# A PSUM bank turn moved on by one, and a small DMA issued earlier, in a fused Fourier-mixing and GELU kernel

## The chip, the core and the metric

The kernel runs on one core of a Trainium2 chip. The metric is the device time of one execution in microseconds. The median of several executions is given; one further execution was recorded by the hardware profiler, and all times inside the kernel are from that one.

## The reference

Two blocks stand one behind the other. The first takes, for each of 8 batches, a two-dimensional Fourier transform of a 3008 by 256 array and keeps the real part. The second multiplies each of the 24064 rows by a 256 by 2048 matrix, applies the quick GELU and multiplies by a 2048 by 256 matrix. All is in 32-bit floating point.

```python
batch, seq, dim = (8, 3008, 256)
n_tokens, d_model, d_ff = (24064, 256, 2048)

X = np.fft.fft(x, axis=1)
X = np.fft.fft(X, axis=2)
attn = X.real.astype(np.float32)

h = attn.reshape(B * S, D) @ w_in
g = h * (1.0 / (1.0 + np.exp(-1.702 * h)))
return (g @ w_out).astype(np.float32)
```

## The kernel before, in words

**The mathematics as tiled.** The transform along the sequence (3008 = 47 × 64) is made in two stages of small matrix products. The first stage (`mix_first` for batch 0, `mix1` for later ones) leaves its results in DRAM, from where `fill` brings them back. The second stage (`stage2`) makes blocks `pq` of cosine and sine parts. The transform along the feature axis is folded into the first weight matrix: `fold_w(n)` multiplies a quarter of it (`wst`) by a cosine and sine matrix and copies the two products from PSUM into a quarter of `wcs[0]` and `wcs[1]`. The second weight matrix is kept in `wo`, with differences of its blocks in `wt`. One row of each block, the Nyquist row `nb`, is handled apart: row 0 of `wcs[1]` holds its weights. `first_row(n)` copies these into columns `af1` and `af2`, and in the later steps row 0 of `wcs[1]` has to be zero. `no_row(c0)` writes 1024 zeros there with a DMA from a table in DRAM (L497).

**Steps.** After an opening written out line by line (L839 to L918) a single loop runs over steps t (L977). A step is one batch, block, half block and pair of hidden columns; NP = 8 pairs make a group. The first eight steps (t < 8) have a form of their own: `hidden(t)` computes two PSUM banks, `pa` (with the cosine weights) and `pb` (sine weights), ScalarE copies `pa` to SBUF, VectorE's `rows(t)` makes sums and differences from both (L566, L569, L557; L557 is the last reader of `pa`), ScalarE's `activate(t)` applies GELU, and `product(t)` multiplies by the second weights three steps later into the banks o0 and o1. `product` and most other matrix products are issued by the helper `halves`, L184, so their lines in the profile are told apart by tile names: `o` the products, `psw` of `fold_w`, `psf` of `first_row`, `psr` of `rotate`, `psn` of `nyquist`. From t = 8 on `begin(t, cs)` takes the place of `hidden`, into a tile `x`, and `begin(t, 1)` reads `wcs[1]` with its row 0.

**The weights' preparation.** In the opening and in the first steps the weights, which come as 64-bit numbers, are turned into 32-bit ones, quarter by quarter: `squares`, `low_up`, `low_down` on ScalarE (L410, L420, L425), `clamp` on POOL (L415), `high` on VectorE (L443 to L445), `finish_in` and `finish_out` on POOL (L457, L465). `differences` (L475) is on POOL, `small_weights` (L687) on VectorE. This stands between the work of the steps on the same engines.

**PSUM.** [...] Two, o0 and o1, hold the products. The other six are handed out by `bank`: without a tag it takes the first of the list `spare` and puts it at the end, so that a bank comes round after six calls. The list starts as b0, b1, b2, o2, o3, o4. A call has to wait until the readers of the bank's former contents are done. At t = NP − 3 = 5 the turn is broken: `spare` is cut down to the banks whose names begin with o, in their present order, and b2 (L980), and `hidden(5)` takes b0 for `pa` and b1 for `pb` by name (L523). From t = 7 on `middle(t)` takes b0 or b1 by name.

**Order of calls around the change.** In the opening: `warm(3)`, `fold_w(0)` (two banks), `warm(1)`, `rotate`, `stage2(0, 0)` (two banks), `first_row(0)`, `fold_w(1)` (two). In the loop: two banks for each `hidden(t)`; one for `nyquist` at t = 0; one for `first_row` at t = 1, 4 and 6; two for `fold_w(2)` at t = 3 and `fold_w(3)` at t = 5; one for `rotate` at the end of t = 4.

**Queues.** [...] SP's queue issues most DMAs. At the end of step 3 it gets, from the list `extra`, `load_matrices` (four DMAs of the first stage's matrices, L324), three `turn`s (DRAM to DRAM, for batch 1) and four calls of `load_x` (two DMAs each, L205), which fill the tile `xt` that `fold1` on POOL first reads at t = 11. In step 4 it then gets `no_row(0)`. `no_row(1024)` follows in step 7.

Of the kernel before, what the change touches and what calls it, by code (L numbers as in the profile page):

```python
# [112 lines left out]
def kernel(ctx: ExitStack, tc, x, w_in, w_out, tab1, tab2, out):  # L113
# [53 lines left out]
    spare = ["b0", "b1", "b2", "o2", "o3", "o4"]  # L167

    def bank(name, tag=None):
        if tag is None:  # L170
            tag = spare.pop(0)
            spare.append(tag)
        if tag in ("o0", "o1"):
            return o_banks[int(tag[1])]
        return (rest if tag[0] == "o" else psp).tile([128, 512], F32, tag=tag, name=name)
# [5 lines left out]
    def halves(out, lhs, rhs, **how):  # L181

        for c0 in (0, 64):
            nc.tensor.matmul(out[c0:c0 + 64], lhsT=lhs[:, c0:c0 + 64], rhs=rhs, skip_group_check=True, **how)  # L184
# [164 lines left out]
    def stage2(b, blk):  # L349

        pq, t4 = pqp.tile([128, 2, 512], F32, tag="pq", name="pq"), t4t[b]
        pqt[b, blk] = pq
        m = m2 if b else m2f
        ps = [bank("ps2") for _ in range(NU)]
        for cs in range(2):
            for h in range(2):
                for g in range(4):
                    for u in range(NU):
                        rows, at = slice(64 * u, 64 * u + 64), cs * 256 + h * 128
                        nc.tensor.matmul(ps[u][32 * g:32 * g + 32, at:at + 128], lhsT=m[rows, cs, h * RUN:(h + 1) * RUN],  # L360
                                         rhs=t4[rows, 4 * blk:4 * blk + 4, cs * H + 32 * g:cs * H + 32 * g + 32],
                                         start=(cs == h == 0), stop=True, skip_group_check=True)
        for u in range(NU):
            for cs in range(2):

                nc.vector.transpose(free(pq[:], cs * 512 + u * RUN, [256, 2], [NU * RUN, 4], [1, RUN]),
                                    free(ps[u][:], cs * 256, [128, 2], [32, 4], [1, 32]))
# [50 lines left out]
    def low_up(key, lo=0, n=1024):  # L418

        nc.scalar.activation(pre[key][2][:, lo:lo + n].bitcast(F32), raw[key][:, lo:lo + n, 0], ACTF.Copy, scale=2.0 ** -29,  # L420
                             bias=2.0 ** 23)

    def low_down(key, lo=0, n=1024):
        r = pre[key][2][:, lo:lo + n]
        nc.scalar.activation(r, r.bitcast(F32), ACTF.Copy, bias=-2.0 ** 23)  # L425

    def bounds(key, end=True):
        prepare(key)
        squares(key, nc.scalar)
        clamp(key)  # L430
        low_up(key)
        if end:
            low_down(key)
# [53 lines left out]
    def first_row(n):  # L487

        ps = bank("psf")
        for f in range(4 * n, 4 * n + 4):  # L490
            halves(ps[:, f:f + 1], wcs[1][0:1, f * 128:f * 128 + 128], twos[:], start=True, stop=True)
        nc.scalar.copy(af2[:, 4 * n:4 * n + 4], ps[:, 4 * n:4 * n + 4])
        nc.scalar.activation(af1[:, 4 * n:4 * n + 4], ps[:, 4 * n:4 * n + 4], ACTF.Copy, scale=0.5)


    def no_row(c0):
        nc.sync.dma_start(out=wcs[1][0:1, c0:c0 + 1024], in_=tab1[127:128, n0 + 4:n0 + 1028])  # L497
# [22 lines left out]
    def hidden(t):  # L520

        n = width(t)
        pa, pb = (bank(name, f"b{i}" if t == NP - 3 else None) for i, name in enumerate(("pa", "pb")))  # L523
        for ps, cs in ((pa, 0), (pb, 1)):
            for i in range(2):
                halves(ps[:, i * 256:i * 256 + n], *operands(t, cs, i), start=(i == 0), stop=(i == 1))
        v = sp.tile([128, 512], F32, tag="v", name="v")
        nc.scalar.copy(two(v[:], n), two(pa[:], n))
        vb[t] = v, pa, pb
# [47 lines left out]
    def middle(t):  # L577

        b, blk, hh, p = steps[t]
        n = width(t)  # L580
        x = xb[t] = bank("x", f"b{t % 2}")
        for i in range(2):
            f = 2 * p + i
            nc.scalar.activation(x[:, i * 256:i * 256 + n], nbt[b, blk][:, hh * 256:hh * 256 + n], ACTF.Copy,  # L584
                                 scale=af1[:, f:f + 1])

    def begin(t, cs=0):

        n = width(t)
        for i in range(2):  # L590
            halves(xb[t][:, i * 256:i * 256 + n], *operands(t, cs, i), start=False, stop=(cs == 1))
# [315 lines left out]
    squares(out0, nc.scalar)  # L907
    stage2(0, 0)
    first_row(0)
    low_up(out0)  # L910
    low_down(out0)
    high(out0)
# [9 lines left out]
    def at(t, fn, *args):  # L922
        extra.setdefault(t, []).append((fn, args))
# [9 lines left out]
    rows_at = {1: 1, 4: 2, 6: 3}  # L933
    for t, c in ((0, 2), (1, 3)):
        at(t, load_out, c, nc.sync)
    at(3, load_matrices)
    if B > 1:
        for k in range(3):
# [38 lines left out]
    for t in range(n + LAG):  # L977
        if t < NP:
            if t == NP - 3:
                spare[:] = [tag for tag in spare if tag[0] == "o"] + ["b2"]  # L980
            if t == NP - 1:
                middle(NP)
            hidden(t)
            if t == NP - 1:
                begin(NP)
                no_row(1024)
            if t == 4:
                no_row(0)
            if t == 0:
                low_up(in2)  # L990
                nyquist(0, 0)
                low_down(in2)
            if t in rows_at:
                first_row(rows_at[t])
            if t >= LAG and t != LAG + 1:
                product(t - LAG, 0, None)
            if t == LAG:
                product(1, 0, None)
            if t == 5:
                bounds(("out", 2))  # L1000
            if t == 6:
                low_down(("out", 3))
            if t:
                activate(t - 1)
            if t == 3:
                bounds(("in", 3))
            if t == 5:
                bounds(("out", 3), False)
            if t in early:
                fold_w(early[t])  # L1010
            rows(t)
            if t == NP - 1:
                doubled(NP)
                middle(NP + 1)
        else:
            after, special = (any(fn in (mix1, stage2) for fn, _ in extra.get(k, ())) for k in (t - 1, t))
            if t < n:
                begin(t, 1)
            if t == NP:
                activate(t - 1)  # L1020
            if t < n:
                forward(t)
            if after and t + 1 < n:
                middle(t + 1)
            opening = (t - LAG) % NP == 0 and t >= NP + LAG
            one, other = (t - LAG, (1, 2, 4, 7)), (t - LAG - 1, (5, 6, 3))
            if opening:
                small_products(*other)
            cut = 0 if opening and not after else 3 if after else 2
            product(t - LAG, 0, cut)  # L1030
            if after:
                small_products(one[0], one[1][:1])
                small_products(other[0], () if opening else other[1][:1])
            if t + 1 < n:
                begin(t + 1)
            if not opening:
                small_products(other[0], other[1][after:])
            product(t - LAG, cut, 6 if t - LAG == last else None)
            small_products(one[0], one[1][after:])
            swap(t - LAG - 2)  # L1040
            if t < n:
                backward(t)
            if t + 1 < n:
                doubled(t + 1)
            if t < n:
                activate_back(t)
                sums(t, nc.gpsimd)
            if t + 2 < n and not special:
                middle(t + 2)
            combine_small(t - LAG - 1)  # L1050
            if t - LAG == last:
                product(last, 6, None)
            sums(t - 1, nc.vector)
            deeper(t - 2, 0)
            deeper(t - 3, 1)
        if t == NP:
            psu.close()
            low = ctx.enter_context(tc.tile_pool(name="low", bufs=1, space=PS))
            pot["low"] = low.tile([128, 3 * 512], F32, tag="low", name="low")
        if t >= LAG:  # L1060
            combine(t - LAG)
            combine_last(t - LAG - 2)
            turn_last(t - LAG - 3, 0)
            turn_last(t - LAG - 4, 1)
        if t >= NP:
            spare[:] = [f"b{t % 2}"] * special + ["b2"]
        for fn, args in extra.get(t, ()):
            fn(*args)
# [28 lines left out]
```

## Time and profile before

| what | us |
|---|---|
| median of 3 runs | 1861.46 (1861.33 to 1863.06) |
| the profiled execution | 1861.87 |
| its span, first to last instruction | 1860.1 |
| TensorE working (99% of the span) | 1842.7 |
| VectorE working (82%) | 1516.6 |
| ScalarE working (62%) | 1145.5 |
| POOL working (52%) | 966.8 |
| mean granted clock of TensorE | 0.997 of full |

The span leaves out 1.8 us that lie around the first and the last instruction. In the profile PE is TensorE's matmuls and PEld its loads of weights, DVE is VectorE, ACT ScalarE, POOL GpSimd and SP the engine that issues DMAs. A line such as "o<-big,wo" names the tile written and the tiles read. In a list of waits, "PE pb L184 <- DVE t L347: 2.6, 1, 2.6" says that matmuls into `pb` waited for an instruction of VectorE at line 347 for 2.6 us in total, once, the longest 2.6. Matmuls are pipelined and their ends are modelled, so the distance from one start to the next is the better measure of what a group costs. The eight first steps lie between 38.9 and about 88 us of the span.

### The profile page before, as it was taken

Reading aid. Unit: us, or ns where it says so; the run is one execution under the profiler, and the core shown is the slowest. Engines: PE = TensorE matmul, PEld = TensorE weight load, DVE = VectorE, ACT = ScalarE, POOL = GpSimd, SP = SyncE. Lnnn points to the kernel's source line nnn. Section 1 sums busy time; section 2 is a strip of 40 time slices with the busy share of each in tenths; the row PEclk is TensorE's granted clock in tenths of the full one; section 3 lists DMA queues with packets and bytes.
Section 4 is the critical chain, followed back from the end, with each engine's and each line's share of the span. In section 5 each row is a group of like instructions: output and inputs, shape, how many; then the busy total and the mean of one; then the engine's idle time right before and its main releaser. Section 6 shows DMA issues by size and latency. Waiting matters only on the chain.

```text
span 1860.1 us, 56075 instructions
## 1 busy us (share of the span) xinstructions
PE 1842.7 (99%) x23718; PEld 1402.6 (75%) x23718; DVE 1516.6 (82%) x2222; ACT 1145.5 (62%) x2240; POOL 966.8 (52%) x1053
## 2 busy tenths in 40 slices
PE   8999999999999999999999999999999999999998
PEld 4577777777777777777777777777777777778776
DVE  6778788888788877987789878888888888878874
ACT  5656665666666566666665666656666666656663
POOL 4676345844367443773347643486445754434442
PEclk9999999999999999999999999999999999999999
DMA  8721340224112250113302232021411111100111
GB/s 285 175 61 34 78 74 19 63 57 95 26 27 64 57 93 19 52 45 86 65 13 57 52 86 52 17 77 35 101 31 25 36 46 36 31 19 13 23 20 24
DMA packets 149691, 105.31 MB, mean 57 GB/s; under 512 B 106041, under 2 KB 130649, under 8 KB 148880
## 3 DMA queue, kind: packets, MB, share of 16 engines
q1 hardware_dynamic: 146608, 99.68, 23.4%
q8 instruction: 187, 3.06, 0.7%
q10 hardware_dynamic: 2832, 2.05, 0.4%
q14 instruction: 64, 0.52, 0.1%
HBM read 64.41 MB, written 48.05 MB: 60 GB/s over the span
## 4 chain that ended last, share of the span: by engine, by line
PE 91%; DVE 4%; POOL 2%; ACT 1%; DMA 1%; issue 1%; SPq 0%; DVEq 0%; ACTq 0%; POOLq 0%
PE x L184 33%; PE o L184 25%; PE low L677 24%; PE o L677 4%; PE ps L255 2%; PE ps L360 1%; DVE big L643 1%; DVE big L443 1%; ACT x L584 1%; DMA xt<-in_x_dram 1%; DMA big<-in_moe_w_in_dram 0%; DVE big L444 0%; DVE big L557 0%; DVE big L778 0%; PE po L184 0%
## 5 line engine op out<-in xcount | busy, mean ns | idle before, releaser
L614 POOL TENSOR_TENSOR big<-big 128x256 f32<-128x256 f32 (+1 forms) x376 | 347.6, 925 | 832.6 <-ACT big L606 714.0
L184 PE MATMUL x<-pq,wcs 128*64 128x256 f32 (+1 forms) x6016 | 771.4, 377 | 1.2 <-ACT x L584 0.3
L643 DVE TENSOR_TENSOR big<-big 128x512 f32<-128x512 f32 (+1 forms) x736 | 623.8, 862 | 31.3 <-PE low L677 14.4
L184 PE MATMUL o<-big,wo 128*64 128x256 f32 (+1 forms) x4800 | 622.8, 376 | 0.0
L184 PEld LDWEIGHTS x<-pq,wcs 128*64 128x64 f32 x6016 | 409.7, 137 | 191.5 <-issue 15.0
L184 PEld LDWEIGHTS o<-big,wo 128*64 128x64 f32 x4800 | 343.0, 137 | 148.8 <-issue 1.8
L596 ACT ACTIVATE g<-x 128x512 f32<-128x512 f32 (+1 forms) x376 | 221.7, 590 | 373.8 <-PE x L184 372.5
L557 DVE TENSOR_TENSOR big<-g,x 128x512 f32<-128x512 f32 (+2 forms) x440 | 253.7, 588 | 196.8 <-ACT big L599 196.3
L677 PE MATMUL low<-big 128*64 128x128 f32 (+1 forms) x5888 | 382.8, 270 | 0.0
L584 ACT ACTIVATE x<-nb,af 128x256 f32<-128x256 f32 (+1 forms) x752 | 352.7, 469 | 12.2
L677 PEld LDWEIGHTS low<-big 128*64 128x64 f32 x5888 | 337.5, 137 | 29.2
L615 POOL TENSOR_TENSOR big<-big 128x256 f32<-128x256 f32 (+1 forms) x376 | 359.1, 955 | 0.0
L599 ACT ACTIVATE big<-x 128x512 f32<-128x512 f32 (+1 forms) x376 | 220.4, 586 | 198.7 <-PE x L184 169.3
L606 ACT ACTIVATE big<-big 128x512 f32<-128x512 f32 (+1 forms) x376 | 231.9, 617 | 40.5 <-DVE big L557 38.7
L677 PE MATMUL low<-big,wo 128*64 128x128 f32 (+1 forms) x2944 | 220.2, 270 | 0.1
L677 PEld LDWEIGHTS low<-big,wo 128*64 128x64 f32 x2944 | 171.6, 137 | 3.2 <-DVE big L643 0.4
L622 DVE TENSOR_TENSOR big<-big 128x512 f32<-128x512 f32 (+1 forms) x188 | 157.6, 838 | 6.5
L621 DVE TENSOR_TENSOR big<-big 128x512 f32<-128x512 f32 (+1 forms) x188 | 136.4, 725 | 5.5 <-POOL big L614 5.5
L778 DVE TENSOR_TENSOR big<-big,low 128x512 f32<-128x512 f32 (+3 forms) x184 | 109.1, 610 | 3.5
L677 PEld LDWEIGHTS o<-big,wo 128*64 128x64 f32 x1472 | 92.2, 137 | 25.0
L677 PE MATMUL o<-big,wo 128*64 128x128 f32 (+1 forms) x1472 | 110.0, 270 | 0.0
L227 POOL TENSOR_TENSOR xt<-xt 111x510 f32<-111x510 f32 x56 | 81.0, 1447 | 4.4
(95 smaller groups left out, 959.5 us busy)
## 6 DMA issues: line engine op xcount, KB each, us to landing
out_dram<-os SPq DMA_DIRECT2D x284, 64.0 KB
t<-Td SPq DMA_DIRECT2D x22, 512.0 KB
Td<-xt SPq DMA_DIRECT2D x56, 192.0 KB
xt<-in_x_dram SPq DMA_DIRECT2D x14, 512.0 KB
xt<-Xr SPq DMA_DIRECT2D x14, 512.0 KB
nb<-Nd SPq DMA_DIRECT2D x23, 256.0 KB
out_dram<-os SPq DMA_DIRECT2D x96, 56.0 KB
Xr<-in_x_dram SPq DMA_DIRECT2D x7, 752.0 KB
```

The source lines that it names most:

```text
L184: nc.tensor.matmul(out[c0:c0 + 64], lhsT=lhs[:, c0:c0 + 64], rhs=rhs, skip_group_check=True, **how)
L557: nc.vector.tensor_tensor(free(out, at + m - 1, [by, 2], [RUN, blocks], [-1, m]), *ins, op=op)
L584: nc.scalar.activation(x[:, i * 256:i * 256 + n], nbt[b, blk][:, hh * 256:hh * 256 + n], ACTF.Copy, scale=af1[:, f:f + 1])
L596: nc.scalar.activation(two(g[:], n), two(xb[t][:], n), ACTF.Copy, scale=2.0)
L599: nc.scalar.activation(front(t), two(xb[t][:], width(t)), ACTF.Gelu_apprx_sigmoid)
L606: nc.scalar.activation(back(t), back(t), ACTF.Gelu_apprx_sigmoid)
L614: eng.tensor_tensor(right(t, S1, n), left(t, A21, n), right(t, A22, n), op=ALU.add)
L615: eng.tensor_tensor(left(t, S3, n), left(t, A11, n), left(t, A21, n), op=ALU.subtract)
L621: eng.tensor_tensor(s2, s1, a11, op=ALU.subtract)
L622: eng.tensor_tensor(s4, a12, s2, op=ALU.subtract)
L643: nc.vector.tensor_tensor(out, i0, i1, op=how)
L677: nc.tensor.matmul(o, lhsT=lhs, rhs=rhs, start=first_in, stop=(p == NP - 2), skip_group_check=True)
```

## The change

Two things are changed in the kernel. Behind `first_row(0)` in the opening, the first entry of `spare` is put at its end without being used, so that each later call takes the bank one place further on. And `no_row(0)` is no longer called in step 4 but put on the list of step 3, ahead of `load_matrices`.

```diff
     squares(out0, nc.scalar)
     stage2(0, 0)
     first_row(0)
+    spare.append(spare.pop(0))
     low_up(out0)
     low_down(out0)
     high(out0)
...
     for t, c in ((0, 2), (1, 3)):
         at(t, load_out, c, nc.sync)
+    at(3, no_row, 0)
     at(3, load_matrices)
     if B > 1:
         for k in range(3):
...
             if t == NP - 1:
                 begin(NP)
                 no_row(1024)
-            if t == 4:
-                no_row(0)
             if t == 0:
                 low_up(in2)
                 nyquist(0, 0)
```

## The prediction

> **What bounds the kernel now.** I read the page's engine table first, then TensorE's waits over the whole run, then the chain of waits, the order of time and the clock by stretches around the one place that these lead to.
>
> ```profile
> span 1860.1 us, 56075 instructions
> PE 1842.7 (99%) x23718; PEld 1402.6 (75%) x23718; DVE 1516.6 (82%) x2222; ACT 1145.5 (62%) x2240; POOL 966.8 (52%) x1053
> ...
> PE ps L312 <- DVE first L292: 3.0, 2, 2.3
> PE warm L330 <- DVE wcs L843: 2.7, 1, 2.7
> PE pb L184 <- DVE t L347: 2.6, 1, 2.6
> PE psw L184 <- POOL wst L457: 0.9, 2, 0.5
> PE pa L184 <- ACT af L493: 0.4, 1, 0.4
> PE x L184 <- ACT x L584: 0.3, 2, 0.2
> ```
>
> TensorE bounds the kernel: it works for 99% of the span, and all that it waits is these few lines, some 10 us. Behind 66 us only the last line (0.3 us) is left. So what TensorE loses in the opening is never caught up, and what it gains there should reach the end. Of the three large waits, two lie before 15 us and wait for the first input. The third, 2.6 us in one piece, ends at 64.70 us:
>
> ```profile
> 61.05 1.06 PE L184 MATMUL pa<-pq,wcs 128*64 128x256 f32 x8
> 64.70 1.97 PE L184 MATMUL pb<-pq,wcs 128*64 128x256 f32 x8 [2.59 <-DVE t L347]
> 66.44 5.61 PE L184 MATMUL o<-big,wo 128*64 128x256 f32 x32
> ...
> 77.73 3.67 PE L184 MATMUL o<-big,wo 128*64 128x256 f32 x32
> ...
> 63.00:63.20 0.20, 0.00 (x0) 0.00 (x0) 0.20 (x2) 0.20 (x1) 0.20 (x1) 1.00 0.16 41
> 63.80:64.20 0.40, 0.00 (x0) 0.00 (x0) 0.37 (x2) 0.40 (x1) 0.40 (x1) 0.50 0.03 5
> 69.70:70.00 0.30, 0.30 (x4) 0.15 (x2) 0.30 (x1) 0.00 (x0) 0.30 (x1) 0.50 1.08 109
> 70.40:70.60 0.20, 0.20 (x6) 0.14 (x4) 0.17 (x2) 0.00 (x0) 0.20 (x1) 0.92 0.85 82
> ```
>
> The first four lines are TensorE in order of time (start, length). The others are stretches: length, then the busy time of PE, PEld, DVE, ACT and POOL, then the granted clock. During the wait the clock falls to 0.50 and comes back only at about 70.4 us. The same 32 product matmuls take 5.4 us behind the wait and 3.5 us later. The wait costs about twice what the list of waits says.
>
> **Which wait it is.** This is step t=5, `hidden(5)`: `pa` ran, `pb` waited. I wrote out the turn of `spare` by hand. Before the change, the calls of step 4 take b1 and b2 (`hidden(4)`), o2 (`first_row(2)`) and o3 (`rotate`). `hidden(5)` has its banks fixed by name: b0 for `pa`, b1 for `pb`. So `pb` of step 5 goes into the bank of `pa` of step 4, whose last reader is `rows(4)`'s reversed sum, L557, on VectorE:
>
> ```profile
> 61.23 1.22 DVE L445 SCALAR_TENSOR_TENSOR big<-big 128x1024 uint32<-128x1024 uint32 x1
> 62.37 0.68 DVE L566 TENSOR_TENSOR big<-v,pb 128x512 f32<-128x512 f32 x1
> 62.97 0.86 DVE L569 SCALAR_TENSOR_TENSOR dif<-nb,af,pb 128x256 f32<-128x256 f32 x2
> 63.87 0.69 DVE L557 TENSOR_TENSOR big<-pa,dif 128x512 f32<-128x512 f32 x1
> 64.47 0.16 DVE L347 COPY t<-psr 128x8 f32<-128x8 f32 x1
> ```
>
> L557 ends at 64.56 and the weight load of `pb` starts at 64.67, 0.11 us later. The profile names L347, which ended last (64.63), but that copy reads o3, which `pb` doesn't touch. The same 0.11 us stands between `rows(0)`'s L557 (end 44.50) and `hidden(2)`'s weight load (44.61), where there is no L347.
>
> [...] everything behind `pb` stands too, though `product(2)` needs nothing that is late. [...] 1.6 us of idling (62.0 to 63.6) sufficed, and it took 5.7 us of work to get it back. [...]
>
> **The bank turn, step by step.** One `pop` and `append` costs no instruction. Written out, step 4 now takes b2, o2, o3, o4, and `fold_w(2)` of step 3 has b0 and b1. Both banks of `hidden(5)` were then last read by that fold's copies to SBUF, which end at 58.42 and 59.28. `pa` and `pb` need not wait.
> - Idling: `pb` would start a group's time (0.87 us) after `pa`, at 61.92, instead of 64.70: 2.78 us.
> - `pb` itself: 64.70 to 66.44 is 1.74 us, at full clock 0.87: 0.87 us.
> - `product(2)`: 66.44 to 71.87 is 5.43 us; the same at 77.73 took 3.51 and at 83.73 3.45, mean 3.48: 1.95 us.
>
> The sum is 5.60 us. A check: 5.7 us of work at clock 0.50 lose 2.85, against 0.87 + 1.95 = 2.82.
>
> Six other allocations get other predecessors, and none waits. `fold_w(1)` (34.81) takes banks of `warm` and of `rotate`, copied by 33.45. `hidden(0)` takes the banks of `stage2`, whose transposes it needs anyhow. The Nyquist row (40.75) takes `first_row(0)`'s, read by 35.57, and `pa` of `hidden(1)` takes `fold_w(0)`'s, read by 32.6. All the other places keep their predecessor of six places before, the 0.39 us wait at 44.65 included. The first bank of `fold_w(3)` now waits for `pb` of step 4, read by L569 until 63.83. `hidden(6)`'s second waits for `pa` of step 4 (64.56).
>
> **What is late next.** TensorE arrives 5.6 us earlier, and each supplier must keep up:
> - `product(2)` at 62.79: activations done by 53.4, weights (`finish_out(1)`) by 59.3.
> - `fold_w(3)` at 66.27: needs `wst` from POOL (L457), ready at 65.00 whatever TensorE does. Slack 1.27 us. Its bank has 2.4.
> - `hidden(6)` at 69.70: needs ScalarE's copies of `fold_w(3)`. ScalarE works without a gap from 61.03 to 68.96, then idles 5.71 us. The copy would be wanted at 74.66 − 5.60 = 69.06. Slack 0.10 us, the tightest of all. If it is missed, it costs what is missed, say 0.3 us, with no loss of clock.
> - `product(4)` at 78.1: weights from POOL's `finish_out(2)`, which can follow `differences(0)` at 71.07 and end by 73.6.
> - `finish_out(3)` can start at 77.4, as POOL is free from 76.5.
> - VectorE begins `rows(5)` at 64.63, as soon as it is free, instead of 66.78, and then waits for `hidden(6)` as before.
>
> From t=6 on every engine idles for TensorE (4.49 us VectorE, 5.71 ScalarE, 4.61 POOL), so their work moves with it.
>
> **The zeros.** The 4 KB DMA of `no_row(0)` costs TensorE nothing by itself. It moves on SP's queue from behind `load_x` (issued at 67.88) to ahead of `load_matrices` (48.20), past the four matrix loads, three `turn`s and four `load_x` calls (eight DMAs). It has to wait until `hidden(3)`'s `pb` matmuls have read the row, about 48.32. So SP waits 0.12 us and issues for 0.3: all behind it is issued some 0.4 to 0.6 us later. The next that need it are `fold1` on POOL at 109.35 (103.7 after the change), while DMA traffic fades out at about 81. So it is hidden by 20 us. The reader of the zeros is `begin(8, 1)`: at 87.18 before, at 81.58 after. Left in its old place, the row would stand behind the loads of x that fade out at 81, with under 1 us to spare. Bounds: I cost the move at 0, its worth as a guard is 0 to 1 us, and its harm at most 0.6 us if a load did matter. Nothing is moved past on POOL's queue.
>
> **The sum.** The profiled execution took 1861.87 us (span 1860.1): minus 5.60 gives 1856.27. The median of the runs is 1861.46, 0.41 lower: 1855.86. I say 1856.0. About 0.2% (3.7 us) can be told from no change.
>
> **Rivals.**
> - A, the sum above: 1856.0, own range 1855.1 to 1857.0 (0.3 us at ScalarE's copy, 0.6 us at the loads, a little less from the 0.3 us waits). Chance 0.86.
> - B, the wait goes and the half clock stays, or a late supplier returns as much: then only 2.78 us is won, 1856.0 + 2.82 = 1858.8. [...] Against: 0.50 appears only inside this wait and until 70.4; neighbours at 0.39 to 0.50 us kept 1.00. Chance 0.06.
> - C, no gain: the named releaser L347 is the true one, and `pb` still stands until 64.7: 1861.5. For it: the name and 0.04 us between its end and the load. Against: the banks, and the 0.11 us seen twice. Chance 0.03.
> - D, slower: TensorE runs into `fold_w(3)` before `wst` is there, because POOL's L457, now beside other VectorE work, ends late. A stall of s there costs s, and once it is some 1.6 us long it brings its own half clock, 2.85. The gain is used up when s + 2.85 passes 5.6, that is, s over 2.75, L457 over 4.0 us late; 5 us late gives 1861.46 + 0.98 = 1862.4, and from 7.7 us late (s = 6.45) the loss can be told from no change. Against: only 0.4 us of L457 now lies beside `rows(5)`. Chance 0.05.
>
> **How the numbers follow.** A's range, widened towards B and by the 1.7 us over which the runs spread, gives 1854.9 to 1858.2, leaving out most of B, C and D. Faster over 0.2% is A and the little of B that wins more than its 2.78 us (which lies within 0.2%): 0.86 + 0.02 = 0.88. Within: C, the rest of B and 0.02 of D, 0.03 + 0.04 + 0.02 = 0.09. Slower: the rest of D, 0.03.
>
> **What would show it.** In the profile after, the list of TensorE's waits lacks the 2.6 us line, the clock stays at 1.00 between 62 and 71 us, `product(2)` starts near 62.8 and takes 3.5, and the last `x` groups of the opening come 5.6 us earlier. SP's L497 stands ahead of L324, near 48.4. The forecast is wrong if a new TensorE wait over 1 us stands at `psw` or `pa` near 66 to 70 us, or if the gain is seen at 80 us and lost by the end.

## The result, and the profile after

| what | before | after |
|---|---|---|
| median of 12 runs each, us | 1861.15 (1860.58 to 1863.06) | 1857.03 (1855.82 to 1858.42) |
| the profiled execution, us | 1861.87 | 1857.22 |
| its span, us | 1860.1 | 1855.4 |

The medians differ by 4.1 us or 0.22%; the ratio is 0.9977 (95% interval 0.9968 to 0.9986), so the changed kernel is faster. TensorE's waits over the whole span of the changed kernel, in the same columns as before:

```profile
PE ps L312 <- DVE first L292: 2.9, 1, 2.9
PE warm L330 <- DVE wcs L843: 2.7, 1, 2.7
PE psw L184 <- POOL wst L457: 1.3, 3, 0.5
PE pa L184 <- ACT af L493: 0.4, 1, 0.4
PE x L184 <- ACT x L584: 0.4, 2, 0.2
```

The 2.6 us of `pb` are gone and nothing over 0.5 us has come in their place. TensorE and SP follow in order of time, then one stretch (length, busy time of PE, PEld, DVE, ACT and POOL, the granted clock, the busy share of the DMA engines, GB/s). The clock was 1.00 in each of the ten stretches of 1 us from 62 to 72 us:

```profile
62.01 1.06 PE L184 MATMUL pa<-pq,wcs 128*64 128x256 f32 x8
62.90 1.03 PE L184 MATMUL pb<-pq,wcs 128*64 128x256 f32 x8
63.77 3.62 PE L184 MATMUL o<-big,wo 128*64 128x256 f32 x32
67.22 3.60 PE L184 MATMUL psw<-wst,small 128*64 128x512 f32 x16
...
76.59 1.03 PE L184 MATMUL pa<-pq,wcs 128*64 128x256 f32 x8
...
49.31 0.28 SPq L497 DMA_DIRECT2D wcs<-in_tab_dram  x1
49.65 1.69 SPq L324 DMA_DIRECT2D w<-in_tab_dram  x4
...
66.00:67.00 1.00, 1.00 (x12) 0.64 (x10) 0.99 (x3) 1.00 (x2) 1.00 (x1) 1.00 1.00 303
```

From `pa` of step 5 to `pa` of step 7 it is 76.59 − 62.01 = 14.58 us. Before, the second of these started 81.24 − 61.05 = 20.19 us behind the first:

```profile
81.24 1.03 PE L184 MATMUL pa<-pq,wcs 128*64 128x256 f32 x8
```

The difference is 5.61 us, the prediction's 5.60. But the spans differ by 4.7 and the medians by 4.1. For the first gap, look at VectorE's first work on the weights, before and after:

```profile
21.69 1.23 DVE L412 TENSOR_TENSOR big<-big 128x1024 f32<-128x1024 f32 x1 [1.79 <-DMA big<-in_moe_w_in_dram]
```
```profile
22.62 1.23 DVE L412 TENSOR_TENSOR big<-big 128x1024 f32<-128x1024 f32 x1 [1.78 <-DMA big<-in_moe_w_in_dram]
```

The first quarter of the weights landed 0.93 us later in the profile after, and all behind it moved along. The change issues nothing so early. In ten profiles this start lies between 21.56 (filled3) and 22.80 us (row_only), 22.43 in a second profile of the kernel before, so it is how executions differ. The second gap, 5.6 us in two profiles against 4.1 us in the medians, is what the experiments had to explain.

### The profile page after: what moved, and what is told of

It is laid out like the page before. It is cut to its first block, busy times and chain, and to the rows that moved or that the text cites. A ratio compares the mean times of both kernels' runs of the same rounds, so it can differ in the third digit from the quotient of the medians.

```text
span 1855.4 us, 56074 instructions
## 1 busy us (share of the span) xinstructions
PE 1840.3 (99%) x23718; PEld 1400.7 (75%) x23718; DVE 1521.0 (82%) x2222; ACT 1146.7 (62%) x2240; POOL 972.2 (52%) x1053
## 4 chain that ended last, share of the span: by engine, by line
PE 92%; DVE 3%; POOL 2%; ACT 1%; DMA 1%; issue 1%; SPq 0%; DVEq 0%; POOLq 0%; ACTq 0%
PE x L184 33%; PE o L184 26%; PE low L677 24%; PE o L677 4%; PE ps L255 2%; PE ps L360 1%; DVE big L643 1%; DMA xt<-in_x_dram 1%; ACT x L584 1%; PE psw L184 0%; PE pa L184 0%; DMA big<-in_moe_w_in_dram 0%; DVE big L778 0%; PE po L184 0%; PE pb L184 0%
```

## The experiments

Theory 1 is the prediction's. The other theories are stated in the expectations. Five rounds were timed for each kernel, with the kernel before beside it on the same chip. Its medians were 1861.26 in the first four, 1861.49 in the next four and 1861.45 in the last three.

| run | median, us | against before (95% interval of the ratio) |
|---|---|---|
| turn_only | 1858.68 | 0.9984 to 0.9997 |
| row_only | 1861.77 | 0.9992 to 1.0008 |
| filled5 | 1861.40 | 0.9992 to 1.0009 |
| before_again | 1861.14 | 0.9992 to 1.0008 |
| filled3 | 1860.26 | 0.9985 to 1.0001 |
| swapped | 1862.37 | 0.9998 to 1.0014 |
| act_row | 1857.61 | 0.9971 to 0.9987 |
| best | 1857.15 | 0.9965 to 0.9985 |
| after_again | 1856.88 | 0.9965 to 0.9985 |
| best_again | 1856.85 | 0.9965 to 0.9985 |
| filled1 | 1859.64 | 0.9984 to 1.0000 |

**turn_only: the bank turn without the earlier zeros.**

```diff
     first_row(0)
+    spare.append(spare.pop(0))
     low_up(out0)
```

> The bank turn alone, the zeros left in step 4. Theory 1 (the turn carries the whole gain: 2.8 us of idling and 2.8 us of half clock at pb of step 5): 1857.0 us, as the full change, within 0.5; no TensorE wait over 0.5 us behind 16 us. Theory 2 (the earlier zeros are needed once TensorE is early): a wait of 0 to 1 us at the first x matmuls that read the sine weights, near 82 us, 1857.0 to 1858.0.

Measured: 1858.68, which is 2.58 us under the kernel before beside it, where the full change won 4.12. TensorE in order of time, its waits behind 66 us, and two stretches in columns as above:

```profile
78.69 3.62 PE L184 MATMUL o<-big,wo 128*64 128x256 f32 x32
84.20 0.98 PE L184 MATMUL x<-pq,wcs 128*64 128x226 f32 x8 [1.89 <-DMA wcs<-in_tab_dram]
...
PE x L184 <- DMA wcs<-in_tab_dram: 1.9, 1, 1.9
...
82.00:83.00 1.00, 0.31 (x4) 0.00 (x0) 0.97 (x2) 0.64 (x1) 1.00 (x1) 1.00 0.78 78
83.00:84.00 1.00, 0.00 (x0) 0.00 (x0) 1.00 (x2) 0.00 (x0) 1.00 (x2) 1.00 0.09 8
```

The wait of `pb` is gone with the turn alone, but `begin(8, 1)` now waits 1.9 us for the zeros, which SP issued at 70.2 behind the loads of x. The matmuls start only when the DMA engines, busy to 83 us, have run empty. Theory 2 was right in its place; its size, "0 to 1", was too small. Zeros that come early enough are what makes the turn's gain whole. Five of the 21 executions lie at 1860.56 to 1861.62 and the others under 1859.4. Those five may have lost clock behind the new wait as well; the profiled one did not, so this is not shown.

**row_only: the earlier zeros without the turn.**

```diff
+    at(3, no_row, 0)
     at(3, load_matrices)
...
-            if t == 4:
-                no_row(0)
```

> The earlier zeros alone, the bank turn as before. Theory 1: 1861.2 us, as before, with the 2.6 us wait of pb and the half clock behind it as they were. Theory 3 (holding SP for the zeros delays the loads behind it, and this is what brings the gain down from 5.6 to 4.1 us): 1862 to 1863 us.

No difference from before is seen (1861.77 against 1861.26, the interval holds 1), and the profile has the 2.6 us wait of `pb` again. While TensorE is late, nobody needs the zeros early. Theory 3 needs some 1.5 us, 5.6 less 4.1, and the interval just reaches that far. But in the full profile after, no engine waits for the loads behind the zeros, and act_row below speaks against it.

**act_row: the turn, the zeros in step 4 but from ScalarE's queue.**

```diff
     def no_row(c0):
-        nc.sync.dma_start(out=wcs[1][0:1, c0:c0 + 1024], in_=tab1[127:128, n0 + 4:n0 + 1028])
+        (nc.sync if c0 else nc.scalar).dma_start(out=wcs[1][0:1, c0:c0 + 1024], in_=tab1[127:128, n0 + 4:n0 + 1028])
...
     first_row(0)
+    spare.append(spare.pop(0))
     low_up(out0)
```

> The bank turn, with the zeros left in step 4 but issued from ScalarE's queue instead of SP's. If the zeros were late because they stood behind the loads of x in SP's own rings: they land within some us, no wait of x for them, 1857.0 us as the full change. If any DMA is late while the 16 engines are full with loads: a wait of 1 to 2 us at x again, 1858.7.

`x` does not wait for the zeros, and the median is 1857.61. They were late because of where they stood on SP's queue. This run doesn't tell apart whether SP's wait at `load_x` or the transfers ahead of them did it: ScalarE issued at 59.8, SP in turn_only at 70.2. The run also speaks against Theory 3: SP isn't held for the zeros here, and yet the gain is 3.9 us and not 5.6.

**before_again: the kernel before, as a control.**

> The kernel before, unchanged, as a control with a profile of its own. Theory 1: 1861.2 us; the wait of pb near 2.6 us and product of step 2 at half clock again. Theory 4 (the depth of the loss at half clock varies from run to run, so that the gain over many runs is less than in the one profile): the 5.4 us of that product are shorter in this profile, between 3.5 and 5.4.

Its `pb` waits 2.60 us as ever, but the loss behind it is another:

```profile
65.51 1.08 PE L184 MATMUL pb<-pq,wcs 128*64 128x256 f32 x8 [2.60 <-DVE t L347]
66.40 5.34 PE L184 MATMUL o<-big,wo 128*64 128x256 f32 x32
71.54 3.63 PE L184 MATMUL psw<-wst,small 128*64 128x512 f32 x16
...
66.00:66.50 0.50, 0.50 (x8) 0.41 (x6) 0.00 (x0) 0.50 (x1) 0.50 (x1) 1.00 0.69 213
67.00:67.50 0.50, 0.50 (x6) 0.37 (x4) 0.50 (x2) 0.50 (x1) 0.50 (x2) 0.50 1.11 246
70.50:71.00 0.50, 0.50 (x8) 0.41 (x6) 0.50 (x1) 0.00 (x0) 0.50 (x2) 1.00 1.21 123
```

Here the clock fell only at 66.6, when `pb` had already run, and was back at 70.05. `pb` took 0.89 and the product 5.14: 0.02 + 1.66 = 1.7 us lost, against 2.8 in the first profile. Theory 4 holds in its first part: the same wait costs different amounts in two executions.

**filled5, filled3, filled1: the wait filled with work.** The edit is filled3's; the others make five calls or one.

```diff
         for ps, cs in ((pa, 0), (pb, 1)):
+            if t == NP - 3 and cs:
+                idle = bank("warm", spare[0])
+                for _ in range(3):
+                    nc.tensor.matmul(idle[:], lhsT=wcs[0][:, 0:128], rhs=wcs[0][:, 0:512], start=True, stop=True)
```

> The kernel before, with five dummy matmuls of 0.47 us each between pa and pb of step 5, into a bank that is free then; their results are thrown away. The wait for the bank stays (pb still starts at about 64.7), but TensorE works through most of it. Theory 1: the clock stays at 1.00, pb and the product behind it take 0.87 and 3.5 us, and the time falls by 2.8 us to about 1858.4. If the half clock came from something else than the idling: no gain, 1861.2.

```profile
61.90 1.06 PE L184 MATMUL pa<-pq,wcs 128*64 128x256 f32 x8
62.89 4.56 PE L528 MATMUL warm<-wcs 128*128 128x512 f32 x10
67.38 1.08 PE L184 MATMUL pb<-pq,wcs 128*64 128x256 f32 x8
```

filled5 missed by its own design. A dummy call makes two matmul records and takes 0.9 us, not 0.47, so five of them ran to 67.4, beyond the wait. `pb` started 5.48 us behind `pa`, against 3.65 in the profile before: 1.83 us later. In this profile `pb` and the product took 0.92 and 3.45 us, so no half clock, and the median is 0.14 us over before. So what was saved at half clock is about what the delay cost, some 1.7 us. That is an estimate, since the 1.83 us are from one profile.

> As filled5, with three dummy calls, since one call takes 0.9 us and not 0.47: 2.7 us, so that the wait of pb (2.8 us) is filled but not lengthened. Only the loss at half clock goes. Theory 1 (that loss is 2.8 us in every execution, as in the profile before): 1858.4 us. Theory 4 (it varies with where the wait falls, 1.7 us in the control's profile, and is some 1.3 us on the average, 4.1 measured less 2.8 of idling): 1859.9 us. In its profile pb starts near 65, with the clock at 1.00.

```profile
60.87 1.06 PE L184 MATMUL pa<-pq,wcs 128*64 128x256 f32 x8
61.87 2.84 PE L528 MATMUL warm<-wcs 128*128 128x512 f32 x6
64.64 1.08 PE L184 MATMUL pb<-pq,wcs 128*64 128x256 f32 x8
65.55 3.62 PE L184 MATMUL o<-big,wo 128*64 128x256 f32 x32
69.00 3.60 PE L184 MATMUL psw<-wst,small 128*64 128x512 f32 x16
```

`pb` starts 3.77 us behind `pa`, 0.12 later than in the profile before, but it and the product take 0.91 and 3.45 us: no half clock. The median falls by 1.23 us, not by 2.8. The interval just reaches 1, so the size is rough.

> As filled3 with one dummy call (0.9 us), so that 1.9 us of the wait of pb stay idle. If 1.9 us of idling never bring the half clock: as filled3, 1860.3 us. If they bring it as 2.8 us do: 1861.4 us, as before. Between: in some executions only.

Eleven of its 13 runs lie from 1859.17 to 1860.39, two at 1861.43 and 1862.51. Its median is 1.81 us under before. That suggests that 1.9 us of idling mostly leave the clock alone, though no profile shows such an execution. The profiled one is the slowest: VectorE was late there, `pb` waited 2.5 us, and the clock did fall:

```profile
66.41 1.44 PE L184 MATMUL pb<-pq,wcs 128*64 128x256 f32 x8 [2.47 <-DVE t L347]
67.00:67.50 0.50, 0.50 (x6) 0.34 (x4) 0.00 (x0) 0.50 (x1) 0.50 (x1) 0.50 1.05 250
```

Every execution also has its mean granted clock on record, rounded to 0.001. Over 109 executions of the kernel before its mean is 0.9976, over the 39 of filled5, filled3 and filled1 0.9984, and over the 50 of the five runs that wait neither for the bank nor for the zeros (after, act_row, best, after_again, best_again) 0.9984 too. So filling the wait brings the clock back as removing it does. The difference, 0.00076 before rounding, makes 1.4 us of full clock in 1860 us. This estimate counts half clock during idling as well.

**swapped: a longer wait.**

```diff
-        pa, pb = (bank(name, f"b{i}" if t == NP - 3 else None) for i, name in enumerate(("pa", "pb")))
+        pa, pb = (bank(name, f"b{1 - i}" if t == NP - 3 else None) for i, name in enumerate(("pa", "pb")))
```

> The kernel before with the two named banks of step 5 exchanged: pa takes b1 (the bank of step 4's pa) and waits, pb follows without a wait. The wait begins 0.87 us earlier and ends at the same instant, so it is 3.65 us instead of 2.78, and pa's 0.87 us come behind it. Theory 1 (fixed loss at half clock): 1861.2 + 0.9 = 1862.1 us. Theory 4 (a longer wait makes the half clock certain and deep in every execution): 1861.2 + 0.9 + 1.5 = 1863.6 us, with at least 2.8 us lost at half clock in the profile.

Measured: 1862.37, 0.88 us over before, though the interval just holds 1. That is Theory 1's number. Theory 4's second part, that a longer wait makes the loss certain and deep, falls as to the depth: in the profile 3.5 us of waiting cost 0.76 us in `pb` and 0.90 in the product, 1.7 again. Whether the loss comes in every execution, one profile can't show.

```profile
64.74 1.08 PE L184 MATMUL pa<-pq,wcs 128*64 128x256 f32 x8 [3.50 <-DVE t L347]
65.62 1.91 PE L184 MATMUL pb<-pq,wcs 128*64 128x256 f32 x8
67.25 4.57 PE L184 MATMUL o<-big,wo 128*64 128x256 f32 x32
```

**best, best_again: one more wait away.** The Nyquist row takes o0, the skip goes, and the list is set once:

```diff
-    spare.append(spare.pop(0))
...
-        ps = bank("psn")
+        ps = bank("psn", "o0")
...
+            if t == 3:
+                spare[:] = ["b0", "b1", "o3", "o4", "o2", "b2"]
```

> The full change with another turn: the Nyquist row's bank is o0, which is free before the products begin, no skip behind the first second stage, and in step 3 the list is set so that fold_w of that step takes b0 and b1. Besides the wait of pb of step 5 this takes away the 0.41 us wait of pa of step 2 (near 45 us), which stood for the bank of step 0's pa. Theory 1: no TensorE wait of pa or pb is left, 1857.0 - 0.4 = 1856.6 us. Rival: VectorE or POOL, which were level with TensorE there, take the 0.4 us back before 70 us, 1857.0.

> The changed kernel again, beside the kernel of run best on the same chip: 1857.0 us; the gain over the kernel before 4.1 us again (2.8 us of idling and on the average 1.2 to 1.4 us at half clock).

> The kernel of run best again, beside the changed one. If the 0.41 us that pa of step 2 no longer waits reach the end: 0.4 us under after_again, 1856.6. If they are given back later: equal within 0.2 us.

The wait of `pa` of step 2 is gone, and the medians are equal (1856.85 and 1856.88). Part of the gain is handed back at step 10, where `x` waits for ScalarE, first in after_again, then in best_again:

```profile
90.72 0.98 PE L184 MATMUL x<-pq,wcs 128*64 128x226 f32 x8 [0.18 <-ACT x L584]
```
```profile
91.21 0.98 PE L184 MATMUL x<-pq,wcs 128*64 128x226 f32 x8 [0.49 <-ACT x L584]
```

That returns 0.3 of 0.4 to 0.5 us; what is left is under what these runs can tell. No version was found that beats the changed kernel.

## Why the prediction was right, point by point

- **Which wait, and that the turn removes it: right.** It stood for the bank and not for L347: in the changed kernel L347 ends at 65.62 and `pb` starts at 62.90. Rivals B, C and D did not come about.
- **Idling, 2.78 us: right.** From `pa` to `pb` of step 5 it is 3.65 us in the profile before and 0.89 after, 2.76 less. filled1, where the wait stays and the half clock seems mostly absent, lies 2.76 us over after_again on the same chip (1859.64 − 1856.88).
- **Half clock, 0.87 + 1.95 = 2.82 us: the mis-sized term of the sum.** It was read from one profile, which was a bad case. Over many executions the loss is 1.2 us (filled3), 1.4 (the recorded clocks), 1.7 (filled5) or 1.8 (filled1). With 2.8 of idling that makes 4.0 to 4.6; measured are 4.1 and, in after_again, 4.6. The upper end is no check of its own: filled1's 1.81 and the 2.76 above add up to after_again's gain by construction. The forecast of 1856.0 was 1.0 us too low for this reason. The 1857.03 lies just above Rival A's own range, which ended at 1857.0. The stated range, to 1858.2, held it because it had been widened towards B and by the spread of the runs, not because the varying loss was foreseen; that much is luck.
- **What is late next: right.** ScalarE's copies for `hidden(6)` followed the engine's earlier work without a gap in the profile after, the predicted tightest place, and TensorE did not wait for them.
- **The zeros, "0 to 1 us" as a guard: too small.** Their worth is 1.5 us in the medians (4.12 less 2.58). The step that failed took the loads' fading at about 81 us for fixed, and set it against `begin(8, 1)` at 81.6. That was one profile again, and an early one: the busy share of the DMA engines falls from 0.70 to 0.04 at 81 us there, from 0.74 to 0.11 at 82 us in the profile after, and from 0.78 to 0.09 at 83 us in turn_only. The zeros on SP's queue in step 4 were issued at 67.88 in the profile before and at 70.18 in turn_only, where the matmuls started at 84.2. As the change holds both parts, this did not touch its forecast.
- **The zeros' own cost, 0: no contradiction.** No TensorE wait stands behind the held SP queue, and row_only shows no difference. The 0.4 to 0.6 us by which all behind the zeros was to be issued later fit the matrix loads (48.20 before, 49.65 after, in a profile that lies 0.93 later). They do not fit the last `turn` (52.98, 58.66): the traces put SP's waits ahead of it (1.3 us before, 1.8 and 3.7 us after) down to a transfer of `in_moe_w_out`. Whether the zeros held that transfer up is not shown.

## What to carry to other kernels

When banks are handed out in turn and one place takes banks by name, write the turn out: only the place in the turn decides which late reader the named bank inherits, and moving it costs no instruction (56075 in the profile before, 56074 after). Before pulling an engine ahead, look for small transfers that stand behind large ones on the same queue and were early enough only because the engine was late (here a wait of 1.9 us in turn_only). A loss at half clock should be priced from several profiles of the same kernel, not from one (here 2.8 and 1.7 us), and so should the end of a burst of transfers (here 81 to 83 us).

## What the runs showed of the hardware

The half clock behind the wait of step 5 had two lengths. It lasted 3.4 us in three profiles (before_again 66.64 to 70.05, swapped 65.69 to 69.11, filled1 67.0 to 70.41) and 6.8 us in two (before 63.6 to 70.4, row_only 65.05 to 71.88; edges within a stretch come from its mean clock). The edges of swapped, then of row_only:

```profile
65.50:66.00 0.50, 0.50 (x7) 0.33 (x5) 0.00 (x0) 0.14 (x1) 0.50 (x1) 0.69 0.21 53
69.00:69.50 0.50, 0.50 (x7) 0.41 (x5) 0.47 (x2) 0.50 (x1) 0.50 (x2) 0.89 1.17 123
65.00:65.50 0.50, 0.00 (x0) 0.00 (x0) 0.47 (x1) 0.50 (x1) 0.50 (x1) 0.55 0.33 78
71.50:72.00 0.50, 0.50 (x6) 0.34 (x4) 0.47 (x2) 0.00 (x0) 0.50 (x1) 0.62 1.11 111
```

A mean clock of 0.69 over 0.50 us, for instance, is full clock for 0.19 us and half clock for the rest, so the fall lies at 65.69. In the two long cases the clock fell inside the wait, 1.5 us (before) and 1.8 us (row_only) after its beginning. In the three short ones it fell 1.13 us (before_again), 0.95 (swapped) and 0.59 (filled1) after its end. At half clock `pb` took 1.74 us in the profile before, twice its 0.87. So the same 2.6 us of waiting cost 1.7 us in before_again, where all 3.4 us fell on work, and 2.8 in the profile before, where 5.7 of the 6.8 did. Why the clock fell now inside the wait and now behind it, the traces don't show. So the prediction's 1.6 us of idling and 5.7 us of work are one execution's numbers, and its Rival D, where a stall of 1.6 us brings a loss of 2.85, was an estimate from them. How much idling makes the clock fall stays open: the 1.9 us of turn_only's profile left it at 1.00 up to 88 us, and the times of filled1 suggest the same for most of its executions.

Nor did 0.50 appear "only inside this wait and until 70.4". Both first profiles also have it early, behind TensorE's wait for the first input that ends at 14.4 us (2.28 us before, 2.94 after): from 15.82 to 19.23 us before (mean clocks of 0.82 and 0.77 in the stretches of 0.5 us from 15.5 and 19.0) and from 16.23 to 19.64 after (0.73 and 0.86 from 16.0 and 19.5), 3.4 us again. As both kernels have it, it is no part of the difference.

The 1.4 us lost on the average by the recorded clocks are less than the 1.7 us that 3.4 us at half clock cost. In some executions of the kernel before, the clock may not fall at all, but the estimate is uncertain by some 0.2 us.
